# Four loads of v earlier in the batch, z's bounds in one go at the start, and two small first output units in an attention and soft-MoE kernel

## The chip, the cores and the metric

The kernel runs on one core of one Trainium2 chip. The metric is the device time of one execution in microseconds (us), the median of several runs. The core has a matrix engine (TensorE, PE in the profile, its weight loads PEld), a vector engine (VectorE, DVE), a scalar engine (ScalarE, ACT), GpSimd (POOL) and a queue engine (SyncE, SP) that here issues every DMA of the loop. The profile gives for each stretch the clock that was granted to PE, as a share of full speed.

## The reference

```python
B, S, D, DQK = 8, 2496, 256, 64
scores = z @ z.T / S                      # per batch, 2496 x 2496
attn = maximum(scores, 0) ** 2
x = u * (attn @ v)                        # 8 x 2496 x 256, taken as 19968 x 256

logits = x @ phi                          # 19968 x 32: 8 experts with 4 slots each
d = softmax of logits over the tokens     # columns
slot_input = d.T @ x                      # 32 x 256
h = maximum(slot_input[e] @ w1[e], 0)     # per expert, 256 -> 1024
slot_out[e] = h @ w2[e]                   # 1024 -> 256
c = softmax of logits over the slots      # rows
return c @ slot_out                       # 19968 x 256
```

The scores are symmetric, since keys and queries are both z.

## The kernel before

**Steps.** A batch is worked off in 5 chunks of 512 queries (the last has 448), and each chunk in 10 steps of 256 keys. A batch is so 50 steps; the last batch has its chunks in another order and the last chunk in two parts, 60 steps. A step's scores are made two steps ahead by `prepare`: PE multiplies z with z into `sc`, ACT takes the relu and the square (`r`), a copy to 16-bit floats gives the high part `ph` (on ACT or DVE), and DVE's `r` less `ph` gives the low part `pl`. At the step itself PE adds `ph` and `pl` times the high and low part of v into `acc` (`sums_halves`, `sums_whole`).

**Symmetric blocks.** A block of scores that is needed again transposed is transposed by DVE (`y`), stored to DRAM in four DMAs (`turned<-y`, by `store`) and fetched up to seven steps before its use (`r<-turned`, 1 MB, by `fetch`). A block on the diagonal gives half of itself the same way: `lent<-yd` by `lend`, and `rd<-lent` by `borrow`, at most five steps ahead. For such a step ACT copies the fetched half (`ph<-rd`), DVE makes its low part (`pl<-rd,ph`), and DVE then makes both parts of the other half, which is computed.

**The MoE's first half.** The outputs of two chunks (1024 tokens) make a group: its logits `lg`, and moves `xt<-y` in four times four DMAs of 72 KB that bring the group's x into the form in which PE sums it with the exponentials of the logits (`lg<-xt`). The sums of one group are done with the logits of the next one.

**The queue.** Every engine runs its instructions in the order in which the program is written (`InOrder`, so line L74 stands for nearly all of them in the profile; the tiles' names tell them apart). All DMAs of the loop go out on SP in that order, and the n-th waits until the one eight before it has landed. `transfers(h)` writes them down for step h: the load of u, the fetches that come due, loads of the next batch, and the stores that are due.

**Loads of the next batch.** The table `splits` has the steps at which the next batch's z (five tiles `zr`, each 256 KB) and v (ten tiles `vr`, 256 KB each) are loaded. `v_from` holds v's; `v_sq` and `v_at` hold the steps at which ACT takes the squares of a tile and at which ACT and DVE split it in high and low parts. The numbers are compared with h + 2, so a load with the entry 14 goes out in step 12. Twelve buffers (`NRAW`) hold the raw tiles.

**The opening.** Before the loop, batch 0's z is scaled. `measure_z` takes the sums of squares of some tiles of z on DVE (`sq`, into `tops`), `add_bounds` brings them over all partitions with one matmul into the PSUM tile `idle`, and `factors` makes powers of two of them (`norm`, `z_by`). `raise_z` multiplies a tile of z (`cw` in the profile) by its factor. `measure_v` squares tiles of v with a sum along the row (`vq`, into `energy`). `largest` and `scale_v` make v's factors (`v_by`, `few`) of both, with a matmul `idle<-ident,few`. `keep_busy` issues matmuls whose result nobody reads. `prepare_first` is `prepare` in pieces for the first two steps.

**The tail.** After the last batch, the slots' sums are copied into `sT` (a piece of the tile `tiny`), zeroed around them by GpSimd before; the experts' two layers follow (`layer1`, `layer2`), and `tokens(c, u)` makes a unit of the output: 4 groups of 512 tokens (3 in the last) for one half c of the 256 features, on PE into `pf`, copied by ACT and DVE into `ot` and stored with one DMA (`outT`). `UNITS` lists them; the first half of the features goes through them forwards, the second backwards.

Of the kernel before, what the change touches and what calls it, by code (L numbers as in the profile page):

```python
# [18 lines left out]
P = 128  # L19
B, S, D, DQK = 8, 2496, 256, 64  # L20
N = B * S
E_, SE, FF = 8, 4, 1024
NS = E_ * SE
# [3 lines left out]
NQ = 5  # L27
NG = N // 512
NQG = (NG + 1) // 2
UNITS = [(g, min(4, NG - g)) for g in range(0, NG, 4)]  # L30
ROT = S - QC * (NQ - 1)
NP = KT // 4
NBLK = 16
# [44 lines left out]
def attn_soft_moe_kernel(ctx, tc, uT, v, zz, phi, ww, outT):  # L78
    nc = tc.nc

    pe, act, dve, sp = (InOrder(tc, x) for x in (nc.tensor, nc.scalar, nc.vector, nc.sync))
# [14 lines left out]
    raws = moe.enter_context(tc.tile_pool(name="raws", bufs=1))  # L96
# [11 lines left out]
    def pair(name, n):  # L108
        return [cpool.tile([P, n], F32, name=f"{name}{i}") for i in range(2)]

    tops, norm2, z_by, energy, v_by, out_by, few = (
        pair(name, n)
        for name, n in (("tops", NP), ("norm2", NP), ("z_by", NP), ("energy", 2 * NP), ("v_by", 2 * NP), ("out_by", NP), ("few", 4))
    )
# [55 lines left out]
    def load_v(b, i):  # L170
        raw = raws.tile([P, 2, D], F32, tag="raw", name=f"vr_{b}_{i}", bufs=NRAW)
        sp.dma_start(raw, v[b, :, 2 * i : 2 * i + 2, :])
        by = v_by[b % 2][:, i : i + 1]

        def squares():
            sq = raws.tile([P, 512], BF16, tag="vq", name=f"vq_{b}_{i}", bufs=1)
            act.activation(
                sq, raw.rearrange("p t f -> p (t f)"), AF.Square, accum_out=energy[b % 2][:, i : i + 1]
            )

        def high():
            act.activation(vt_[b, i][:, :, 0], raw, AF.Identity, scale=by)

        def low():
            t = vt_[b, i]
            dve.scalar_tensor_tensor(t[:, :, 1], raw, by, t[:, :, 0], op0=ALU.mult, op1=ALU.subtract)

        return squares, high, low
# [36 lines left out]
    z_splits, v_splits, first_z, first_v = {}, [], [], []  # L225
# [15 lines left out]
    one = cpool.tile([1, 1], F32, name="one")  # L241
# [30 lines left out]
    wa = att.enter_context(tc.tile_pool(name="wa", bufs=2, side="right"))  # L272
# [128 lines left out]
    def prepare_first(k):  # L401


        r = wa.tile([P, 2, QC], F32, tag="r", name=f"r_{k}", bufs=4)
        pend[k] = hi, lo = high_low(k)
        ps, _ = scores(k)

        act.activation(r, ps, AF.Relu, scale=2.0**-22)

        def square():  # L410
            if k:
                act.activation(r, r, AF.Square)
            else:
                dve.tensor_mul(r, r, r)

        def high():
            dve.tensor_copy(hi, r)

        def low():
            dve.tensor_sub(lo, r, hi)  # L420

        return square, high, low

    def prepare(k):

# [452 lines left out]
    for b in range(1, B):  # L878
        base, order = (b - 1) * 2 * NP * NQ, BLOCKS[b == B - 1]
        z_at = [28, 29, 30, 31, 39]  # L880
        v_from = [14, 15, 16, 17, 24, 25, 26, 31, 32, 33]
        v_sq = [17, 18, 19, 20, 28, 29, 30, 33, 34, 35]
        v_at = [47, 42, 43, 44, 45, 46, 48, 49, 50, 51]
        for i, (j, at) in enumerate(zip(order, z_at)):
            splits.setdefault(base + 9 + 2 * i, []).append((load_z, b, j, [base + 12 + 2 * i, base + at]))
        for i, (start, sq, at) in enumerate(zip(v_from, v_sq, v_at)):
            splits.setdefault(base + start, []).append(
                (load_v, b, i, [base + sq, base + at, base + at])
            )
# [73 lines left out]
    def measure_v(n):  # L963
        for _ in range(n):
            first_v.pop(0)()

    def measure_z(js):
        for p in range(*js.indices(NP)):
            first_z[p]()
        add_bounds(0, idle, js)  # L970
        factors(0, idle, js)

    measure_z(slice(0, 1))
    raise_z(0)
    keep_busy(1)
    first = prepare_first(0)
    measure_v(2 * NP)
    measure_z(slice(1, 2))
    raise_z(1)
    for f in first:  # L980
        f()
    keep_busy(3)
    measure_z(slice(2, NP))
    keep_busy(3)
    second = prepare_first(1)
    second[0]()
    keep_busy(3)
    largest(0)
    scale_v(0, idle)
    second[1]()  # L990
    split_first_v()
    second[2]()
    split_first_v()
    for p in range(2, NP):
        raise_z(p)
# [44 lines left out]
    x = xg_.pop(q)  # L1040
    mold, sold = runmax[(q + 1) % 2], slot_acc[(q + 1) % 2]

    tiny = wk.tile([P, 2, 1024], F32, tag="xg", name="tiny").rearrange("p a b -> p (a b)")
    sT = tiny[:, 0:512].rearrange("p (c e k) -> p c e k", c=2, k=NS)
    snew = tiny[:, 512 : 512 + D + 1]
    ET = tiny[:, 1024 : 1024 + P]
    fsel = tiny[:, 1280 : 1280 + 2 * NS].rearrange("p (a s) -> p a s", a=2)
# [3 lines left out]
    apart = tiny[:, 1600 : 1600 + P]  # L1051
    E = wk.tile([P, 2 * P], F32, tag="E", name="E_last", bufs=1)[:, 0:P]
    lt = wk.tile([P, 2 * P], F32, tag="L", name="lt_last", bufs=1)[:, 0:P]
    nc.gpsimd.memset(tiny[:, 0:512], 0.0)

    nc.gpsimd.tensor_scalar(
        apart.rearrange("p (t s) -> p t s", s=NS), ssel.unsqueeze(1).to_broadcast([P, 4, NS]),
# [35 lines left out]
    for t, copy, ps in (2, act.copy, xq[:, 0:D]), (3, dve.tensor_copy, xr[:, 0:D]):  # L1093
# [5 lines left out]
        accum_out=mtop,  # L1099
# [18 lines left out]
    sums = [lg[:, 2 * P : 2 * P + NS], pm[:, 2 * P : 2 * P + NS]]  # L1118
# [21 lines left out]
    dve.tensor_sub(l4, l4, spread(0))  # L1140
    slots(snew, 0)
    for c, copy in enumerate((dve.tensor_copy, act.copy)):
        copy(sT[:, c, :, 0:SE], sums[c].rearrange("p (e s) -> p e s", s=SE))
    act.activation(lt, lt, AF.Exp)
    dve.tensor_reduce(rm[:, 1], l4, axis=AX.X, op=ALU.add)
    dve.tensor_scalar_add(rm[:, 1], rm[:, 1], 1e-9)
# [8 lines left out]
    def layer1(i):  # L1155

        ps = sc_ps.tile([P, 512], F32, tag=sc_ps.name, name=f"h_{i}")
        for a in range(2):
            e = 2 * i + a
            for c in range(2):  # L1160
                for g in range(4):
                    pe.matmul(
                        ps[g * NS : (g + 1) * NS, a * D : (a + 1) * D], sT[:, c, e],
                        w_half(2 * e + c, g // 2)[:, g % 2 * D : (g % 2 + 1) * D],
                        start=(c == 0), stop=(c == 1),
                    )
        act.activation(hidden[:, i], ps, AF.Relu)
        return lambda: dve.transpose(hT[i // 2][:, i % 2].rearrange("p a f s -> p (a f s)"), hidden[:, i])
# [39 lines left out]
    second = rest_ps.tile([P, QC], F32, tag="rest_ps", name="po_second")  # L1208
# [3 lines left out]


    op = ctx.enter_context(tc.tile_pool(name="op", bufs=4, reuse_waits="tile"))
    for i in range(3, len(UNITS)):
        split_hi(i)
        split_lo(i)
    soh = op.tile([P, 2, P], F32R, name="soh", bufs=1)
# [24 lines left out]
    def tokens(c, u):  # L1243
        g0, ng = u
        hi, lo = parts[g0 // 4]
        gs = slice(0, ng)
        ot = op.tile([P, 4, 4, P], F32, tag="ot", name=f"ot_{c}_{g0}")
        pf = []
        for i in range(2):
            ps = ring.pop(0)  # L1250
            ring.append(ps)
            pf.append(ps.tile([P, 2, 4, P], F32, tag=ps.name, name=f"pf_{c}_{g0}_{i}"))
        for m, (a, k) in enumerate(((soh, hi), (soh, lo), (sol, hi))):
            for t in range(4):
                rows = slice(t * NS, (t + 1) * NS)
                pe.matmul(
                    pf[t // 2][:, t % 2, :ng], a[rows, c], k[rows, gs],
                    start=(m == 0), stop=(m == 2), tile_position=(t * NS, 0),
                )
        for tp in range(2):  # L1260
            o = ot[:, :ng, 2 * tp : 2 * tp + 2].rearrange("p g t n -> p t g n")
            (dve.tensor_copy if tp else act.copy)(o, pf[tp][:, :, :ng])
        sp.dma_start(
            outT[c * P : (c + 1) * P, g0 * 512 : (g0 + ng) * 512],
            ot[:, :ng].rearrange("p g t n -> p (g t n)"),
        )
# [8 lines left out]
    first = po[0][:, D : D + P]  # L1275
# [3 lines left out]
    parts_out(0, first)  # L1279
    layer2(1, 0, range(2, 3))  # L1280
    left = [(0, f) for f in range(3, 8)] + [(1, f) for f in range(8)]
    units = [(0, u) for u in UNITS] + [(1, u) for u in UNITS[::-1]]
    for i, (c, u) in enumerate(units):
        if i == 7:
            spread_out(1, slots_out(1), po[1][:, D : D + P])
        tokens(c, u)

        for eg, f in [left.pop(0) for _ in range((3, 0, 0, 1, 2, 3, 4)[i] if i < 7 else 0)]:
            layer2(1, eg, [f])
    att.close()  # L1290

# [42 lines left out]
```

## Time and profile before

| what | us |
|---|---|
| three runs | 1298.11, 1301.54, 1307.86 |
| median | 1301.54 |
| the profiled execution, its own time | 1300.08 |
| its span in the trace | 1298.3 |
| mean granted clock of PE | 0.979 |
| the loop's first `acc` starts at | 20.35 |
| the first `outT` DMA is issued at | 1245.45 |

A page of a profile lists the busy time of each engine with its share of the span, then 40 equal slices of the span with the busy share in tenths. In these, the clock and DMA rows of this kernel are:

```profile
PEclk8999999999999999999999999999999999999985
DMA  4868759784888758785787857978487868899869
```

The page further has the chain of work that ended last, followed back from the end, and groups of instructions. A line of a timeline is the start, the duration, the engine, the line, the operation, the tiles written and read, the shape, how many such instructions stand in a row, and in brackets how long the engine had been idle and what it had waited for. A row of the DMA issues gives the number, the size of one and the median time from issue to landing:

```profile
turned<-y SPq DMA_DIRECT2D x320, 256.0 KB, 5.1
r<-turned SPq DMA_DIRECT2D x76, 1024.0 KB, 7.1
xt<-y SPq DMA_DIRECT2D x288, 72.0 KB, 4.1
vr<-in_v SPq DMA_DIRECT2D x80, 256.0 KB, 5.5
```

### The profile page before, as it was taken

The numbers are of one execution on the slowest core, as the hardware profiler recorded it, in microseconds if no ns is written. First come the engines' busy times: TensorE is split into PE (matmuls) and PEld (weight loads), VectorE is DVE, ScalarE is ACT, GpSimd is POOL, SyncE is SP. The second block draws the span as 40 slices with busy tenths as digits, with TensorE's granted clock in tenths as the row PEclk, the third lists the DMA queues.
The fourth block names the chain that finished last, engine by engine and source line by source line (L and its number), as shares of the span: only waits on it lengthen the run. The fifth ranks groups of instructions, "written<-read, shape, count | busy, mean of one in ns | idle before, by whom it ended". The sixth has DMA issues, their size and how long they took to land.

```text
span 1298.3 us, 27660 instructions
## 1 busy us (share of the span) xinstructions
PE 1253.6 (97%) x10965; PEld 607.7 (47%) x10965; DVE 1100.5 (85%) x1588; ACT 934.6 (72%) x1219; POOL 4.2 (0%) x22
## 2 busy tenths in 40 slices
PE   7999999999999999999999999999999999999984
PEld 3444455445544444344544444344554444445752
DVE  6888899789998899689998899788998899886663
ACT  7877797677867798576977678586886778664553
POOL 1000000000000000000000000000000000000000
PEclk8999999999999999999999999999999999999985
DMA  4868759784888758785787857978487868899869
GB/s 139 234 210 245 231 132 278 232 235 145 212 296 240 250 128 233 259 247 169 167 266 231 272 146 193 294 220 260 110 253 248 267 165 218 261 287 295 309 252 381
DMA packets 136402, 298.88 MB, mean 230 GB/s; under 512 B 17872, under 2 KB 38864, under 8 KB 124240
## 3 DMA queue, kind: packets, MB, share of 16 engines
q1 hardware_dynamic: 136272, 297.11, 74.9%
q8 instruction: 86, 1.41, 0.4%
q14 instruction: 44, 0.36, 0.1%
HBM read 162.04 MB, written 113.77 MB: 212 GB/s over the span
## 4 chain that ended last, share of the span: by engine, by line
PE 81%; ACT 5%; DVE 5%; DMA 5%; issue 2%; SPq 1%; DVEq 0%; ACTq 0%; POOLq 0%
PE acc L74 66%; PE sc L74 10%; ACT r L74 3%; PE lg L74 3%; DVE pl L74 2%; PE pf L74 2%; DVE y L74 1%; DMA r<-turned 1%; ACT ot L74 1%; SPq L74 1%; ACT ph L74 1%; DMA xt<-y 1%; ACT v L74 1%; DMA rd<-lent 1%; PE h L74 1%
## 5 line engine op out<-in xcount | busy, mean ns | idle before, releaser
L74 PE MATMUL acc<-ph,v 64*128 64x512 f16 (+5 forms) x5036 | 931.1, 369 | 3.2 <-DVE ph L74 1.2
L74 PEld LDWEIGHTS <-v 64*128 64x128 f16 (+1 forms) x7554 | 469.7, 95 | 527.7 <-issue 39.5
L74 PE MATMUL acc<-pl,v 64*128 64x512 f16 (+5 forms) x2518 | 602.0, 369 | 2.1 <-DVE pl L74 1.8
L74 DVE TENSOR_TENSOR pl<-r,ph 128x1024 f16<-128x1024 f32 (+1 forms) x410 | 467.5, 1146 | 108.5 <-ACT ph L74 81.4
L74 ACT CAST ph<-r 128x1024 f16<-128x1024 f32 (+1 forms) x286 | 289.7, 1018 | 157.1 <-DMA r<-turned 99.4
L74 ACT ACTIVATE r<-sc 128x1024 f32<-128x1024 f32 (+1 forms) x242 | 229.4, 948 | 125.4 <-PE sc L74 122.8
L74 ACT ACTIVATE r<-r 128x1024 f32<-128x1024 f32 (+1 forms) x241 | 237.4, 985 | 6.8
L74 DVE STREAM_TRANSPOSE y<-r 128x1024 f32<-128x1024 f32 x160 | 198.0, 1238 | 0.0
L74 PE MATMUL sc<-z,z 64*128 64x512 f16 x912 | 124.3, 377 | 1.8 <-ACT r L74 1.5
L74 PEld LDWEIGHTS <-z 64*128 64x128 f16 x1380 | 70.2, 94 | 75.9 <-issue 5.8
L74 DVE CAST ph<-r 128x1024 f16<-128x1024 f32 (+1 forms) x124 | 73.9, 596 | 15.5 <-ACT r L74 15.2
L74 DVE SCALAR_TENSOR_TENSOR xg<-acc,out_by,ut 128x1024 f32<-128x1024 f32 (+7 forms) x57 | 51.7, 930 | 11.0 <-PE acc L74 11.0
L74 DVE SCALAR_TENSOR_TENSOR v<-vr,v_by,v 128x512 f16<-128x512 f32 x80 | 58.0, 725 | 0.0
L74 ACT ACTIVATE v<-vr,v_by 128x512 f16<-128x512 f32 x80 | 57.0, 715 | 0.0
L74 PE MATMUL sc<-z 64*128 64x512 f16 (+1 forms) x468 | 50.6, 321 | 0.0
L74 ACT ACTIVATE vq<-vr 128x512 bf16<-128x512 f32 x80 | 49.8, 623 | 0.3
L74 DVE STREAM_TRANSPOSE y<-xg 128x512 f32<-128x512 f32 x72 | 49.4, 687 | 0.0
L74 DVE COPY ot<-pf 128x1024 f32<-128x1024 f32 (+1 forms) x20 | 24.0, 1198 | 20.6 <-PE pf L74 19.8
L74 ACT COPY ot<-pf 128x1024 f32<-128x1024 f32 (+1 forms) x20 | 19.8, 991 | 24.8 <-PE pf L74 20.7
L74 DVE TENSOR_TENSOR pl<-rd,ph 128x512 f16<-128x512 f32 x36 | 24.0, 667 | 10.9 <-ACT ph L74 10.7
L74 ACT CAST ph<-rd 128x512 f16<-128x512 f32 x36 | 21.8, 607 | 13.9 <-DMA rd<-lent 13.7
L74 PE MATMUL lg<-xt 64*32 64x256 f32 x576 | 21.6, 391 | 5.9 <-DMA xt<-y 5.9
(185 smaller groups left out, 536.0 us busy)
## 6 DMA issues: line engine op xcount, KB each, us to landing
turned<-y SPq DMA_DIRECT2D x320, 256.0 KB, 5.1
r<-turned SPq DMA_DIRECT2D x76, 1024.0 KB, 7.1
xt<-y SPq DMA_DIRECT2D x288, 72.0 KB, 4.1
vr<-in_v SPq DMA_DIRECT2D x80, 256.0 KB, 5.5
outT<-ot SPq DMA_DIRECT2D x18, 1024.0 KB, 6.9
ut<-in_uT SPq DMA_DIRECT2D x31, 512.0 KB, 6.2
lent<-yd SPq DMA_DIRECT2D x144, 64.0 KB, 3.0
rd<-lent SPq DMA_DIRECT2D x36, 256.0 KB, 4.8
```

Source lines behind the costliest of these rows:

```text
L74: return lambda *a, **k: self.tc.keep_in_program_order(f(*a, **k))
```

## The change

Three things are changed.

**Loads.** The first four tiles of v of the next batch are loaded at the entries 6 to 9 of the table in place of 14 to 17, so in steps 4 to 7 of the batch before, not in 12 to 15. Their squares and splits stay where they were.

**Opening.** The relu is a piece of `prepare_first` of its own. The scores of step 1 are issued right after the relu of step 0. The squares of z1 to z4 are taken in one go and go through one matmul of four columns, where there were one of one column and one of three. Nine of the ten tiles of v are squared on ACT and the last on DVE. `keep_busy` is called once with 8 instead of three times with 3.

**Tail.** The first output unit of the first feature half is parted in two: 1 group and 3 groups. `tokens` takes its groups from the right place in the parts of the weights. For the second half the unit stays whole. The matmuls of `layer2` that are written between units are handed on by one place. `sT` becomes two tiles, one for each half of the features: one stays in `tiny`, the other is `apart_s`.

```diff
-UNITS = [(g, min(4, NG - g)) for g in range(0, NG, 4)]
+UNITS = [(0, 1), (1, 3)] + [(g, min(4, NG - g)) for g in range(4, NG, 4)]
...
-        def squares():
-            sq = raws.tile([P, 512], BF16, tag="vq", name=f"vq_{b}_{i}", bufs=1)
-            act.activation(
-                sq, raw.rearrange("p t f -> p (t f)"), AF.Square, accum_out=energy[b % 2][:, i : i + 1]
-            )
+        def squares(engine=act):
+            one, to = raw.rearrange("p t f -> p (t f)"), energy[b % 2][:, i : i + 1]
+            if engine is act:
+                sq = raws.tile([P, 512], BF16, tag="vq", name=f"vq_{b}_{i}", bufs=1)
+                act.activation(sq, one, AF.Square, accum_out=to)
+            else:
+                sq = raws.tile([P, 512], BF16, tag="sq", name=f"vq_{b}_{i}", bufs=1)
+                dve.tensor_tensor_reduce(sq, one, one, 1.0, 0.0, op0=ALU.mult, op1=ALU.add, accum_out=to)
...
-        v_from = [14, 15, 16, 17, 24, 25, 26, 31, 32, 33]
+        v_from = [6, 7, 8, 9, 24, 25, 26, 31, 32, 33]
...
     first = prepare_first(0)
-    measure_v(2 * NP)
-    measure_z(slice(1, 2))
+    first[0]()
+    second = prepare_first(1)
+    measure_v(2 * NP - 1)
+    measure_z(slice(1, NP))
+    for f in first[1:]:
+        f()
+    second[0]()
+    second[1]()
     raise_z(1)
-    for f in first:
-        f()
-    keep_busy(3)
-    measure_z(slice(2, NP))
-    keep_busy(3)
-    second = prepare_first(1)
-    second[0]()
-    keep_busy(3)
+    keep_busy(8)
+    first_v.pop()(dve)
     largest(0)
     scale_v(0, idle)
...
+    apart_s = wa.tile([P, 256], F32, tag="yt", name="apart_s", bufs=1)
     tiny = wk.tile([P, 2, 1024], F32, tag="xg", name="tiny").rearrange("p a b -> p (a b)")
-    sT = tiny[:, 0:512].rearrange("p (c e k) -> p c e k", c=2, k=NS)
+    sT = [tiny[:, 0:256].rearrange("p (e k) -> p e k", k=NS), apart_s.rearrange("p (e k) -> p e k", k=NS)]
...
-        gs = slice(0, ng)
+        gs = slice(g0 % 4, g0 % 4 + ng)
...
-    units = [(0, u) for u in UNITS] + [(1, u) for u in UNITS[::-1]]
+    whole = [(0, 4), *UNITS[2:]]
+    units = [(0, u) for u in UNITS] + [(1, u) for u in whole[::-1]]
     for i, (c, u) in enumerate(units):
-        if i == 7:
+        if i == 8:
             spread_out(1, slots_out(1), po[1][:, D : D + P])
         tokens(c, u)
-        for eg, f in [left.pop(0) for _ in range((3, 0, 0, 1, 2, 3, 4)[i] if i < 7 else 0)]:
+        for eg, f in [left.pop(0) for _ in range((0, 3, 0, 0, 1, 2, 3, 4)[i] if i < 8 else 0)]:
             layer2(1, eg, [f])
```

What this moves is shown at three places. The numbers at the end of names count tiles and differ between the two kernels. The first place is SP in batch 3, steps 14 to 21, the stretch that ends with the last moves of `xt`. Before:

```order
L74 DMA r_6673<-turned_0_2_6196 128x2048
L74 DMA zr_3_6675<-in_zz 128x512
L74 DMA vr_1_6677<-in_v 128x512
L74 DMA turned_1_4_6679<-y_6557 32x4x512 x4
L74 DMA vr_2_6721<-in_v 128x512
L74 DMA xt<-y_6275 32x576 x4
L74 DMA r_6770<-turned_1_2_6575 128x2048
L74 DMA zr_4_6772<-in_zz 128x512
L74 DMA vr_3_6774<-in_v 128x512
L74 DMA turned_1_3_6776<-y_6657 32x4x512 x4
L74 DMA xt<-y_6275 32x576 x4
```

After:

```order
L74 DMA r_6673<-turned_0_2_6190 128x2048
L74 DMA zr_3_6675<-in_zz 128x512
L74 DMA turned_1_4_6677<-y_6559 32x4x512 x4
L74 DMA xt<-y_6286 32x576 x4
L74 DMA r_6766<-turned_1_2_6577 128x2048
L74 DMA zr_4_6768<-in_zz 128x512
L74 DMA turned_1_3_6770<-y_6657 32x4x512 x4
L74 DMA xt<-y_6286 32x576 x4
```

Three loads `vr` are gone from among them; the fourth, `vr_0`, stood a few rows earlier. The second place is SP in batch 2, steps 5 to 11, to which loads come. Before:

```order
L74 DMA rd_4263<-lent_0_3987 128x512
L74 DMA xt<-y_3864 32x576 x4
L74 DMA turned_0_3_4310<-y_4201 32x4x512 x4
L74 DMA xt<-y_3864 32x576 x4
L74 DMA zr_0_4416<-in_zz 128x512
L74 DMA turned_0_4_4418<-y_4296 32x4x512 x4
L74 DMA lent_1_4462<-yd_4448 32x4x128 x4
L74 DMA zr_1_4509<-in_zz 128x512
```

After:

```order
L74 DMA rd_4257<-lent_0_3981 128x512
L74 DMA vr_0_4274<-in_v 128x512
L74 DMA xt<-y_3858 32x576 x4
L74 DMA vr_1_4321<-in_v 128x512
L74 DMA turned_0_3_4323<-y_4195 32x4x512 x4
L74 DMA xt<-y_3858 32x576 x4
L74 DMA vr_2_4372<-in_v 128x512
L74 DMA zr_0_4416<-in_zz 128x512
L74 DMA vr_3_4418<-in_v 128x512
L74 DMA turned_0_4_4420<-y_4307 32x4x512 x4
L74 DMA lent_1_4464<-yd_4450 32x4x128 x4
L74 DMA zr_1_4511<-in_zz 128x512
```

The fetch `rd` of `lent_1`, which step 17 uses, follows some rows further down in both, so all four loads are now ahead of it. In batches 3 and 5 no `xt` stands among these rows. The third place is PE in the opening, behind the first scores (`sc_203`); the second scores are `sc_210`:

```order
 L74 MATMUL idle<-const-bfloat16-1.0 128x512
 L74 MATMUL sc_203<-cw 128x512 x2
-L74 MATMUL idle<-tops_80,const-float32-1.0 128x1
+L74 MATMUL sc_210<-cw 128x512 x2
+L74 MATMUL idle<-tops_80,const-float32-1.0 128x4
 L74 LDWEIGHTS const-bfloat16-1.0
```

The second scores stand ahead of the one bounds matmul, where they came after the matmul of three columns and six rounds of `keep_busy`.

More of the change, by code (lines that the diff above doesn't have):

```diff
@@ L406, in prepare_first, with relu @@
         ps, _ = scores(k)
-        act.activation(r, ps, AF.Relu, scale=2.0**-22)
+        def relu():
+            act.activation(r, ps, AF.Relu, scale=2.0**-22)
         def square():
@@ L420, in low @@
             dve.tensor_sub(lo, r, hi)
-        return square, high, low
+        return relu, square, high, low
     def prepare(k):
@@ L976, in attn_soft_moe_kernel @@
     first = prepare_first(0)
-    measure_v(2 * NP)
-    measure_z(slice(1, 2))
-    raise_z(1)
-    for f in first:
-        f()
-    keep_busy(3)
-    measure_z(slice(2, NP))
-    keep_busy(3)
-    second = prepare_first(1)
-    second[0]()
-    keep_busy(3)
+    first[0]()
[6 more added lines that the diff above has]
+    second[1]()
+    raise_z(1)
+    keep_busy(8)
+    first_v.pop()(dve)
     largest(0)
     scale_v(0, idle)
-    second[1]()
+    second[2]()
     split_first_v()
-    second[2]()
+    second[3]()
     split_first_v()
@@ L1053, in attn_soft_moe_kernel @@
     lt = wk.tile([P, 2 * P], F32, tag="L", name="lt_last", bufs=1)[:, 0:P]
-    nc.gpsimd.memset(tiny[:, 0:512], 0.0)
+    nc.gpsimd.memset(tiny[:, 0:256], 0.0)
+    nc.gpsimd.memset(apart_s, 0.0)
     nc.gpsimd.tensor_scalar(
@@ L1142, in attn_soft_moe_kernel @@
     for c, copy in enumerate((dve.tensor_copy, act.copy)):
-        copy(sT[:, c, :, 0:SE], sums[c].rearrange("p (e s) -> p e s", s=SE))
+        copy(sT[c][:, :, 0:SE], sums[c].rearrange("p (e s) -> p e s", s=SE))
     act.activation(lt, lt, AF.Exp)
@@ L1162, in layer1 @@
                     pe.matmul(
-                        ps[g * NS : (g + 1) * NS, a * D : (a + 1) * D], sT[:, c, e],
+                        ps[g * NS : (g + 1) * NS, a * D : (a + 1) * D], sT[c][:, e],
                         w_half(2 * e + c, g // 2)[:, g % 2 * D : (g % 2 + 1) * D],
@@ L1214, in attn_soft_moe_kernel @@
     op = ctx.enter_context(tc.tile_pool(name="op", bufs=4, reuse_waits="tile"))
-    for i in range(3, len(UNITS)):
+    for i in range(3, len(UNITS) - 1):
         split_hi(i)
```

## The prediction

> **What bounds the kernel now.** I read the page's engine shares first, then the chain, then PE's waits, then PE's timeline and windows around the long ones.
>
> ```profile
> span 1298.3 us, 27660 instructions
> ...
> PE 1253.6 (97%) x10965; PEld 607.7 (47%) x10965; DVE 1100.5 (85%) x1588; ACT 934.6 (72%) x1219; POOL 4.2 (0%) x22
> PE 81%; ACT 5%; DVE 5%; DMA 5%; issue 2%; SPq 1%; DVEq 0%; ACTq 0%; POOLq 0%
> PE lg L74 <- DMA xt<-y: 5.9, 2, 3.1
> PE idle L74 <- DVE tops L74: 5.3, 2, 4.6
> ```
>
> PE is the bound: 97% of the span, 81% of the chain. The change adds and removes almost no PE work, so it can win only where PE stands still or runs slowly. Two stalls for `xt` make 5.9 us; the opening's wait for the bounds of z (`tops`) makes another 5.3. What follows the two `xt` stalls is seen in PE's timeline (start, duration, idle time before in brackets) and in windows (busy time of PE, PEld, DVE, ACT, POOL, then granted clock, DMA share, GB/s):
>
> ```profile
> 238.92 0.42 PE L74 MATMUL lg<-xt 64*32 64x256 f32 x8
> 297.83 0.42 PE L74 MATMUL lg<-xt 64*32 64x256 f32 x8
> 538.54 1.50 PE L74 MATMUL lg<-xt 64*32 64x256 f32 x32 [3.08 <-DMA xt<-y]
> 599.38 0.42 PE L74 MATMUL lg<-xt 64*32 64x256 f32 x8
> 839.94 2.52 PE L74 MATMUL lg<-xt 64*32 64x256 f32 x32 [2.83 <-DMA xt<-y]
> ...
> 506.00:526.00 20.00, 20.00 (x142) 9.00 (x137) 18.87 (x27) 15.01 (x20) 0.00 (x0) 1.00 0.99 330
> 536.24:539.65 3.41, 1.11 (x32) 0.74 (x32) 2.52 (x5) 2.37 (x4) 0.00 (x0) 1.00 0.87 247
> 539.65:543.06 3.41, 3.41 (x29) 1.15 (x18) 3.20 (x8) 0.00 (x0) 0.00 (x0) 0.50 0.49 156
> ```
>
> The stalls lie in batches 3 and 5, at the same step. The 20 us before the first are DMA-bound (share 0.99). The window with the stall has PE busy 1.11 of 3.41 us, and the next 3.41 us run at clock 0.50. From the stall's end to the next `lg<-xt` takes 599.38 - 538.54 = 60.84 us; the same work in batch 1, which has no such stall, takes 297.83 - 238.92 = 58.91. So each stall costs its own length plus 1.93 us of slow clock.
>
> **The change part by part. The four loads, batches 3 and 5.**
>
> ```profile
> 480.00:502.00 22.00, 22.00 (x212) 9.98 (x207) 21.58 (x32) 19.18 (x23) 0.00 (x0) 1.00 0.74 181
> 518.00:522.00 4.00, 4.00 (x20) 1.83 (x19) 3.90 (x9) 2.58 (x4) 0.00 (x0) 1.00 1.00 353
> 526.00:528.00 2.00, 2.00 (x11) 0.94 (x10) 1.93 (x5) 0.00 (x0) 0.00 (x0) 1.00 0.22 72
> 516.72 1.24 DVE L74 STREAM_TRANSPOSE y<-r 128x1024 f32<-128x1024 f32 x1
> 528.54 0.43 SPq L74 DMA_DIRECT2D vr<-in_v  x1
> 531.57 5.07 SPq L74 DMA_DIRECT2D xt<-y  x4
> ```
>
> Four loads of 256 KB leave the queue ahead of the last `xt`. At 353 GB/s one is 0.74 us, all four 2.97. They go to 480 to 502, where the DMA engines are busy 0.74 of the time. The last stores before `xt` carry a `y` that was transposed by 516.72 + 1.24, more than 10 us before they go out, so nothing but the queue holds that stretch and it can move up whole. The stalls shrink from 3.08 to 0.11 and from 2.83 to 0, and the slow clock after each goes: (2.97 + 1.93) + (2.83 + 1.93) = 9.7. Ends: nothing more can be had than 9.8; at least 1.5 (2 x 0.74, the load at 528.54 alone), if the hole at 526 to 528 (share 0.22) eats what is saved ahead of it. I take 9.7, since the DMA engines are busy 0.99 of the 20 us up to that hole: bytes set its place, and fewer bytes move it up. [...]
>
> **The same loads, other batches.** There the place they go to is not empty.
>
> ```profile
> 334.00:354.00 20.00, 20.00 (x192) 10.60 (x190) 19.00 (x26) 17.83 (x20) 0.00 (x0) 1.00 0.86 214
> 368.20 0.60 ACT L74 CAST ph<-rd 128x512 f16<-128x512 f32 x1
> 371.55 0.65 DVE L74 TENSOR_TENSOR pl<-rd,ph 128x512 f16<-128x512 f32 x1
> 372.57 0.69 DVE L74 TENSOR_TENSOR pl<-r,ph 128x512 f16<-128x512 f32 x1
> 373.82 0.38 PE L74 MATMUL acc<-pl,v 128*128 128x512 f16 x1
> 220.51 0.62 ACT L74 CAST ph<-rd 128x512 f16<-128x512 f32 x1 [1.40 <-DMA rd<-lent]
> 221.55 0.65 DVE L74 TENSOR_TENSOR pl<-rd,ph 128x512 f16<-128x512 f32 x1
> 224.67 0.38 PE L74 MATMUL acc<-pl,v 128*128 128x512 f16 x1
> ```
>
> Behind the new loads on SP stand moves of `xt`, stores `turned`, and the fetch `rd` of a diagonal piece; its readers are ACT `ph<-rd`, DVE `pl<-rd`, DVE's other half and at last PE. The shift of `rd` lies between 0 (a fifth of 20 us is free by the 0.86: 2.8 us) and 2.97 plus four issues of 0.43 = 4.7. I take 2.7, near the loads' own time, because SP takes the next DMA only as earlier ones land. Cover in batch 2: DVE comes 371.55 - 368.80 = 2.75 after ACT is done, and PE takes the second half 373.82 - 373.26 = 0.56 after DVE: 3.31 in all. So no stall there, nor in 4 and 6. Batch 1 has 221.55 - 221.13 = 0.42, and with DVE's other half ending 1.71 after 221.55, as in batch 2, 224.67 - 223.26 = 1.41: 1.83 in all. It loses 2.7 - 1.83 = 0.9 (0 to 2.9). In batch 0 the loads go out ahead of its first fetches too; PE's waits name no DMA there, so I count nothing, on that cover alone. The squares and splits of v stay at their steps, so the earlier arrival itself gains nothing.
>
> **The opening.**
>
> ```profile
> 6.92 1.02 ACT L74 ACTIVATE r<-sc 128x1024 f32<-128x1024 f32 x1 [4.69 <-PE sc L74]
> 7.79 0.49 DVE L74 TENSOR_SCALAR cw<-cw,z_by 128x512 f32<-128x512 f32 x1
> 8.19 1.22 DVE L74 TENSOR_TENSOR r<-r 128x1024 f32<-128x1024 f32 x1
> 10.17 1.23 DVE L74 TENSOR_TENSOR pl<-r,ph 128x1024 f16<-128x1024 f32 x1
> 12.77 0.69 DVE L74 CUSTOM_DVE_ANT_0 sq<-cw 128x512 bf16<-128x512 f32 x1
> 13.52 0.59 PE L74 MATMUL idle<-tops,const-float32-1.0 128*128 128x3 f32 x2 [4.63 <-DVE tops L74]
> 15.49 0.17 DVE L74 TENSOR_SCALAR v_by<-energy 128x10 int32<-128x10 int32 x1 [0.77 <-ACT vq L74]
> 15.60 1.94 PE L74 MATMUL sc<-cw 64*128 64x512 f32 x4
> 18.39 0.29 DVE L74 TENSOR_REDUCE few<-idle 128x2 f32<-128x128 f32 x1 [2.33 <-PE idle L74]
> 20.35 0.39 PE L74 MATMUL acc<-ph,v 64*128 64x512 f16 x2 [0.57 <-ACT v L74]
> ```
>
> Before, `few` has its input late because PE runs the second scores (15.60 to 17.54) ahead of it. Now those follow the first relu: 7.94 + 1.94 = 9.9; the one bounds matmul 0.59 more, 10.5; three small DVE operations, 0.17 each as `v_by` (15.49) and their wait, 0.6, 11.1; square, `ph`, `pl` of half 0 take 11.40 - 8.19 = 3.2, 14.3; raising z1 0.49, 14.8; the last v's square, now DVE's, 0.69 as `sq` and a read of its sum, 15.6. DVE now waits there for the last v's landing, with `v_by` and `few` behind it; ACT had squared that v before 15.49, so it is there by 14.8. So `v_by` starts as at 15.49, but PE is free: three DVE operations (0.5), the matmul and its wait (0.5), and `few` is reduced at 16.7, not 18.39. That is 1.7 off, the first `acc` at 18.65. The keep-busy matmuls (8 rounds in one go for 9 in three) follow the bounds matmul at 10.5 and are done by about 14 (8 pairs of 0.39, as the pair at 20.35), so PE idles some 2 of the next 3.4 us, and a window like that was followed by half clock above. The loop's first us would then lose about 1.1; at even odds I deduct 0.5. Net 1.2 gained (0.3 lost clock wholly and a late v, to 2.4 with the second scores at full clock).
>
> **The tail.**
>
> ```profile
> 1244.17 1.23 DVE L74 COPY ot<-pf 128x1024 f32<-128x1024 f32 x1 [0.78 <-PE pf L74]
> 1245.45 25.18 SPq L74 DMA_DIRECT2D outT<-ot  x12
> 1250.00:1294.00 44.00, 27.87 (x278) 15.43 (x276) 20.59 (x18) 17.15 (x19) 0.00 (x0) 0.62 1.01 418
> ```
>
> The output stream is DMA-bound to the end (1.01 at 418 GB/s), so only its start counts. A 256 KB first unit could go out at most 1.28 earlier (1245.45 - 1244.17), and holds 0.63 us of stream; the next unit, 768 KB, can't be ready before the old first one was, and a further pair of copies stands ahead of it. I take half of 0.63, 0.3 gained (-0.4 to 1.3); the parting of `sT` into two tiles is in it, hidden behind copies of 0.2.
>
> Sum: 9.7 - 0.9 + 1.2 + 0.3 = 10.3 less, from the profiled execution's 1300.08 (its span of 1298.3 and 1.8 around it): 1289.8. That execution lies 1.46 under the median 1301.54; against the median it is 0.9% less.
>
> **The rivals.**
> - The loads cost more where they now stand (slower). If each takes its 256 KB at that stretch's own 214 GB/s, 1.22 us, `rd` comes 4.9 later. Batches 2, 4, 6 stall 4.9 - 3.31 = 1.6 and, if the clock falls behind it, lose 1.93 more; batch 1 loses 3.1 + 1.93. That is 3 x 3.5 + 5.0 = 15.6 against the 0.9 counted: 1304.5. It decides from a shift of 3.8, provided the clock falls each time. Against it: the share there is 0.86, so bytes are not yet the limit.
> - The same without the clock, at a shift of 4.0: 3 x 0.7 + 2.2 = 4.3 against 0.9, 1293.2.
> - The loads are not what holds `xt`: the hole at 526 to 528 stays where it is, only 0.74 comes back per stall, and the clock still falls: 1289.8 + 9.7 - 1.5 = 1298.0. For it: a share of 0.22 in the midst of a full queue. Against it: `xt` is behind all four in one queue.
> - The slow stretches stay without the stalls (or a third reason sets the clock): 3.9 less gained, 1293.7. [...]
>
> **How the numbers follow.** Chances: forecast 0.63; loads not the cause 0.14; shift without clock 0.12; clock unmoved 0.05; slower 0.06. The forecast's own range is 1286.5 to 1291.5 (opening and tail at their good ends; batch 1 at its bad one). To 1298.5 the cases at 1293 and 1298 are in; what is left out is the slower rival and tails. About 1% (1288.5 or 1314.6) is what a measurement of this kernel can tell from no change. The forecast lies 1.3 short of the lower bound; four tenths of its chance fall beyond it, 0.25, and with the noise of three runs I say 0.3 for faster by more than 1%. Slower by more than 1% needs the first rival at its worst: 0.04.
>
> **What would show it.** Right: no wait of `lg` for `xt` over 0.5 us in batches 3 and 5, and granted clock 1.00 through 530 to 545; `ph<-rd` later by 2 to 3 us in even batches with PE not waiting for `pl`; a wait for `pl` under 1 us in batch 1 near 224; the first `acc` near 18.6; the first `outT` about 1 us earlier against the copies' start, its end moved by less than 0.5. Wrong: PE waits for `pl` or `ph` at step 17 of batches 2, 4, 6; a wait for `xt` above 2 us left; half clock in the loop at another place.

## The result, and the profile after

| | before | changed |
|---|---|---|
| median of 20 runs, us | 1301.7 | 1295.66 |
| lowest to highest | 1298.11 to 1308.36 | 1293.92 to 1299.94 |
| ratio | | 0.9944, 95% interval 0.9934 to 0.9954 |
| the profiled execution | 1300.08 | 1299.94 |

The change takes 6.0 us off the median; 11.7 were forecast against the first median, 10.3 against the profiled execution. The profiled execution of the changed kernel was the longest of its 20, so the two profiles hardly differ in span, and what the change does must be read stretch by stretch. The page and PE's waits after:

```profile
span 1298.2 us, 27694 instructions
PE 1260.7 (97%) x10973; PEld 611.3 (47%) x10973; DVE 1100.8 (85%) x1588; ACT 932.1 (72%) x1218; POOL 4.2 (0%) x23
...
PE sc L74 <- ACT r L74: 4.8, 12, 1.1
PE idle L74 <- DVE few L74: 2.0, 1, 2.0
...
PE lg L74 <- DMA xt<-y: 0.9, 1, 0.9
...
PE idle L74 <- DVE tops L74: 0.9, 1, 0.9
```

The wait for `xt` fell from 5.9 us to 0.9, the one for `tops` from 5.3 to 0.9. New are 2.0 for `few`, and the waits for ACT's relu ahead of scores are 4.8 (1.8 before). PE is busy 7.1 us longer with nearly the same work: the two stretches at half clock behind the stalls are gone, but others have come, in the opening and in the tail (below). In PE's timeline (start, duration, ...) and the windows (PE, PEld, DVE, ACT, POOL, granted clock, DMA share, GB/s) the two old stalls now read:

```profile
539.57 0.77 PE L74 MATMUL lg<-xt 64*32 64x256 f32 x9 [0.94 <-DMA xt<-y]
838.89 1.69 PE L74 MATMUL lg<-xt 64*32 64x256 f32 x32
...
526.00:528.00 2.00, 2.00 (x11) 0.88 (x9) 2.00 (x4) 2.00 (x5) 0.00 (x0) 1.00 0.68 221
528.00:530.00 2.00, 2.00 (x12) 0.88 (x9) 1.90 (x6) 0.34 (x2) 0.00 (x0) 1.00 0.34 74
530.00:532.00 2.00, 2.00 (x11) 0.94 (x10) 2.00 (x5) 0.00 (x0) 0.00 (x0) 1.00 0.70 174
537.28:540.70 3.42, 2.48 (x68) 1.22 (x64) 2.37 (x4) 3.39 (x5) 0.00 (x0) 1.00 0.82 216
```

One wait is down to 0.94. The other is no longer listed, though its two steps still take 0.92 too long (the table below). No half clock follows either. Counted from its batch's first `acc`, the first of them starts at 539.57 - 469.15 = 70.42 against 538.54 - 465.97 = 72.57 before: 2.15 earlier, not 2.97. The hole in the DMA engines' work ahead of it is still there and wider (0.68, 0.34 and 0.70 in six microseconds, where it was 0.22 in two, with 0.93 and 0.85 on its sides).

The opening after, in timeline and windows:

```profile
6.11 2.08 PE L74 MATMUL sc<-cw 64*128 64x512 f32 x4 [0.29 <-DVE cw L74]
8.23 1.02 ACT L74 ACTIVATE r<-sc 128x1024 f32<-128x1024 f32 x1 [6.00 <-PE sc L74]
9.31 2.08 PE L74 MATMUL sc<-cw 64*128 64x512 f32 x4 [1.12 <-ACT r L74]
11.31 0.59 PE L74 MATMUL idle<-tops,const-float32-1.0 128*128 128x4 f32 x2
15.94 0.68 DVE L74 CUSTOM_DVE_ANT_0 vq<-vr 128x512 bf16<-128x512 f32 x1
16.74 0.17 DVE L74 TENSOR_SCALAR v_by<-energy 128x10 int32<-128x10 int32 x1
17.46 0.44 PE L74 MATMUL idle<-ident,few 64*128 64x64 f32 x4 [1.97 <-DVE few L74]
17.93 0.29 DVE L74 TENSOR_REDUCE few<-idle 128x2 f32<-128x128 f32 x1 [0.62 <-PE idle L74]
19.68 0.61 PE L74 MATMUL acc<-ph,v 64*128 64x512 f16 x2 [0.70 <-ACT v L74]
...
15.09:18.51 3.42, 1.45 (x12) 0.55 (x8) 2.56 (x10) 2.74 (x5) 0.00 (x0) 1.00 0.02 6
18.51:21.92 3.41, 2.53 (x12) 0.70 (x12) 3.32 (x7) 2.98 (x4) 0.00 (x0) 0.50 0.00 0
21.92:25.33 3.41, 3.30 (x18) 0.91 (x14) 3.41 (x7) 2.60 (x4) 0.00 (x0) 0.50 0.02 5
```

The chain runs as forecast, but the first scores take 2.08 here, and the relu ends at 9.25 instead of 7.94; everything behind is later by about as much (`v_by` 16.74 for 15.6, `few` 17.93 for 16.7, `acc` 19.68 for 18.65). Then PE is idle for 1.97 of a window of 3.41 us, and two windows at half clock follow: the first step takes 5.71, where it took 3.46.

In the other batches and the tail:

```profile
224.37 0.62 ACT L74 CAST ph<-rd 128x512 f16<-128x512 f32 x1 [3.68 <-DMA rd<-lent]
372.44 0.62 ACT L74 CAST ph<-rd 128x512 f16<-128x512 f32 x1 [2.00 <-DMA rd<-lent]
...
437.36 0.82 PE L74 MATMUL sc<-z 64*128 64x512 f16 x6 [0.40 <-ACT r L74]
730.26 0.82 PE L74 MATMUL sc<-z,z 64*128 64x512 f16 x6 [0.76 <-ACT r L74]
...
426.23 1.04 ACT L74 CAST ph<-r 128x1024 f16<-128x1024 f32 x1 [2.25 <-DMA r<-turned]
...
1241.13 49.86 SPq L74 DMA_DIRECT2D outT<-ot  x21
...
1240.00:1244.00 4.00, 3.77 (x52) 2.46 (x52) 1.56 (x3) 1.17 (x2) 0.00 (x0) 0.56 0.19 70
1244.00:1248.00 4.00, 3.32 (x26) 1.86 (x26) 1.23 (x1) 1.13 (x2) 0.00 (x0) 0.50 0.56 229
```

Against the batch's first `acc`, `ph<-rd` comes 51.15 - 48.86 = 2.3 later in batch 1 (batch starts 173.22 and 171.65) and 51.47 - 49.39 = 2.1 later in batch 2 (320.97 and 318.81); batch 1 pays 0.6 and batch 2 nothing at that place. But batches 2 and 4 lose 1.0 and 2.05 at steps 35 to 37, a place that the prediction did not speak of: ACT has waited for a turned block there (2.25 at 426.23), and PE then waits for ACT's relu. In the tail the first `outT` goes out early, and then the DMA engines wait for units that PE makes at half clock.

### The profile page after: what moved, and what is told of

The parts are those of the page before. It is cut to its first block, busy times and chain, and to the rows that moved or that the text cites. A ratio compares the mean times of both kernels' runs of the same rounds, so it can differ in the third digit from the quotient of the medians.

```text
span 1298.2 us, 27694 instructions
## 1 busy us (share of the span) xinstructions
PE 1260.7 (97%) x10973; PEld 611.3 (47%) x10973; DVE 1100.8 (85%) x1588; ACT 932.1 (72%) x1218; POOL 4.2 (0%) x23
## 4 chain that ended last, share of the span: by engine, by line
PE 74%; ACT 8%; DMA 7%; DVE 6%; issue 2%; SPq 2%; ACTq 0%; DVEq 0%; POOLq 0%
PE acc L74 59%; PE sc L74 9%; ACT r L74 4%; PE lg L74 2%; SPq L74 2%; PE pf L74 2%; DMA r<-turned 2%; DVE y L74 2%; DMA turned<-y 2%; DVE pl L74 2%; ACT ph L74 2%; DMA rd<-lent 1%; ACT ot L74 1%; ACT v L74 1%; DMA vr<-in_v 1%
## 5 line engine op out<-in xcount | busy, mean ns | idle before, releaser
L74 DVE COPY ot<-pf 128x1024 f32<-128x1024 f32 (+2 forms) x21 | 24.1, 1149 | 24.8 <-PE pf L74 24.8
L74 ACT COPY ot<-pf 128x1024 f32<-128x1024 f32 (+2 forms) x21 | 20.0, 951 | 28.7 <-PE pf L74 28.7
L74 DVE SCALAR_TENSOR_TENSOR z<-zr,z_by,z 128x512 f16<-128x512 f32 x35 | 25.8, 738 | 0.0
```

The lines of the kernel that those rows point to most:

```text
L74: return lambda *a, **k: self.tc.keep_in_program_order(f(*a, **k))
```

## The experiments

Each kernel was timed in five rounds against the kernel before on the same chip (which took 1301.08 to 1302.25 in these rounds; the 1301.7 belongs to the second row), and profiled once, so the columns behind the median show single executions. This table has the ratios and what the profiled executions show, all in us: the start of the first `acc`; the duration of the first step; what batch 1 and batches 2 and 4 together take above 147.16 each; what steps 21 and 22 of batches 3 and 5 take above the 8.48 of batch 1; and the time from the experts' first layer (`h`) to the last landing of `outT`. Nearly all of what batches 2 and 4 lose lies at steps 35 to 37; only in the run of the loads alone 0.73 of it lies at steps 16 and 17 of batch 4. The loads column says in which batches the four loads go out early.

| kernel | ratio (95%) | median | loads | first acc | step 0 | b 1 | b 2+4 | steps 21, 22 of b 3, b 5 | h to end |
|---|---|---|---|---|---|---|---|---|---|
| before | | 1301.7 | none | 20.35 | 3.46 | 0.0 | 0.0 | 5.23, 4.99 | 67.96 |
| changed | 0.9944 (0.9934 to 0.9954) | 1295.66 | all | 19.68 | 5.71 | 0.59 | 3.07 | 1.50, 0.92 | 71.10 |
| changed, again | 0.9951 (0.9931 to 0.9971) | 1295.37 | all | 19.66 | 5.75 | 1.16 | 4.44 | 1.09, 0.65 | 68.12 |
| loads only | 0.9939 (0.9916 to 0.9962) | 1294.5 | all | 21.72 | 3.46 | 1.46 | 2.89 | 0.74, 1.69 | 68.02 |
| opening only | 1.0002 (0.9987 to 1.0018) | 1301.2 | none | 19.77 | 4.84 | 0.0 | 1.84 | 6.56, 3.54 | 67.94 |
| tail only | 1.0018 (1.0001 to 1.0035) | 1304.38 | none | 21.92 | 3.46 | 0.0 | 0.0 | 3.66, 3.00 | 68.22 |
| loads, all but 3 and 5 | 1.0010 (0.9994 to 1.0026) | 1302.92 | not 3, 5 | 22.39 | 3.46 | 1.23 | 1.04 | 3.36, 1.95 | 67.97 |
| loads, 3 and 5 | 0.9941 (0.9924 to 0.9958) | 1293.04 | 3, 5 | 21.83 | 3.46 | 0.0 | 0.0 | 0.86, 0.30 | 68.00 |
| the same with z | 0.9948 (0.9928 to 0.9969) | 1293.96 | 3, 5 | 20.36 | 3.46 | 0.0 | 1.08 | 0.16, 0.19 | 67.94 |
| opening, 12 rounds | 0.9984 (0.9971 to 0.9996) | 1298.92 | none | 19.63 | 3.46 | 0.0 | 0.0 | 4.90, 4.33 | 68.03 |
| units only | 1.0000 (0.9986 to 1.0014) | 1302.19 | none | 21.74 | 3.46 | 0.0 | 0.0 | 5.43, 6.58 | 68.15 |
| sT only | 1.0001 (0.9985 to 1.0016) | 1302.38 | none | 21.98 | 3.46 | 0.0 | 2.21 | 5.33, 5.60 | 67.99 |
| loads and opening, 12 rounds | 0.9930 (0.9912 to 0.9948) | 1293.08 | all | 19.88 | 3.46 | 1.69 | 0.25 | 0.12, 1.07 | 68.03 |
| loads and z in 3 and 5, opening, 12 rounds | 0.9915 (0.9897 to 0.9932) | 1291.3 | 3, 5 | 19.80 | 3.46 | 0.0 | 0.1 | 0.22, 0.11 | 67.95 |

**The changed kernel again**, with no edit.

> The changed kernel once more. Its profiled execution took 1299.94 us, the longest of its 20 runs (median 1295.66), so another execution is wanted. If what the profile showed at steps 35 to 37 of batches 2 and 4 (1.0 and 2.0 us) belongs to the change, it shows again and the span stays near 1298; if it belongs to that execution, batches 2 and 4 come back to 147.2 each. The ratio to the kernel before should be 0.994 to 0.996 in any case.

The losses in batches 2 and 4 were there again (4.4), and the first step took 5.75; the tail was back at 68.12. So the half clock in the opening and the losses were no chance of one execution. The 3.1 of the tail did not come again.

**Each part alone.** Loads:

```diff
-        v_from = [14, 15, 16, 17, 24, 25, 26, 31, 32, 33]
+        v_from = [6, 7, 8, 9, 24, 25, 26, 31, 32, 33]
```

> Only the four loads moved. My theory: they carry the gain, 7 to 9 us (ratio 0.993 to 0.9945), with the waits for xt in batches 3 and 5 below 1 us and no half clock behind them, and 0.6 lost at step 16 of batch 1. Rival, that the even batches pay for it: waits at steps 35 to 37 of batches 2 and 4, ratio 0.996 or more.

The loads carry the gain: 0.9939, some 7.9 us of 1301. Both waits for `xt` are short (1.10 the longer), no half clock follows, and batch 1 pays 1.46. The losses at steps 35 to 37 that the rival named are there too, 1.11 in batch 2 and 1.05 in batch 4, without the ratio that it gave. Batch 4 loses another 0.73 at steps 16 and 17: there `ph<-rd` comes 3.7 later against the batch's first `acc` than in the kernel before, past the cover of 3.31 that the prediction worked out, and PE waits.

The opening, the diff being the two pieces of the change on `prepare_first` with its calls and on `squares`:

```diff
     first = prepare_first(0)
-    measure_v(2 * NP)
-    measure_z(slice(1, 2))
+    first[0]()
+    second = prepare_first(1)
+    measure_v(2 * NP - 1)
+    measure_z(slice(1, NP))
...
+    keep_busy(8)
+    first_v.pop()(dve)
```

> Only the opening changed. My theory: the first acc comes 0.7 to 1.7 earlier, but PE idles before the loop, the first step runs at half clock and takes some 5.7 us for 3.5, so that nothing is gained or up to 1.5 us lost (ratio 1.000 to 1.0015). Rival, that the half clock was chance of one execution: the first acc 0.7 to 1.7 earlier and the first step 3.5, ratio 0.9985 to 0.9995.

Nothing gained: the first `acc` is early, the first step takes 4.84. The slow first step came another way here than in the two profiles of the changed kernel. In those the clock rose at 15.09 and 15.79 and fell again one window later, with PE idle for 1.97 and 2.06 us of that window. Here it had not risen at all: the second `sc<-cw` of the chain still takes 2.08 at 9.14 and the next 2.06 at 17.74, and the clock is first full at 23.66. This run also had 1.84 in batches 2 and 4, with no load moved.

The tail, with the pieces of the change on `UNITS`, `tokens` and `sT`:

```diff
+UNITS = [(0, 1), (1, 3)] + [(g, min(4, NG - g)) for g in range(4, NG, 4)]
...
+    sT = [tiny[:, 0:256].rearrange("p (e k) -> p e k", k=NS), apart_s.rearrange("p (e k) -> p e k", k=NS)]
```

> Only the first output unit in two and sT in two tiles. My theory: the stream of outT starts 1 us earlier but has a hole behind the small units, and ends where it ended: ratio 0.9995 to 1.0005. Rival, that the earlier start is kept: 0.9990. Rival, that the units bring half clock earlier in the tail: 1.001 to 1.002.

The ratio is above 1, 1.0018; from `h` to the end it is 68.22 against 67.96.

**Where the loads gain and where they cost.** The loads moved in all batches but 3 and 5, then in 3 and 5 alone (the table serves the batch after, so 4 and 6):

```diff
-        v_from = [14, 15, 16, 17, 24, 25, 26, 31, 32, 33]
+        v_from = [*([14, 15, 16, 17] if b in (4, 6) else [6, 7, 8, 9]), 24, 25, 26, 31, 32, 33]
```

> Loads moved in batches 0, 1, 2, 4 and 6, not in 3 and 5. My theory: what these batches lose comes from the moved loads, through fetches that land later: 1.5 at steps 16 and 17 of batch 1, 1.0 to 2.5 at steps 35 to 37 of batch 2, 1.5 to 2.0 in batch 4, and the two stalls for xt stay: ratio 1.002 to 1.004. Rival: the losses at steps 35 to 37 came by chance of the execution (the run with the opening alone had them too): batch 1 loses its 0.6 to 1.5, batches 2 and 4 nothing, ratio 1.000 to 1.001.

```diff
-        v_from = [14, 15, 16, 17, 24, 25, 26, 31, 32, 33]
+        v_from = [*([6, 7, 8, 9] if b in (4, 6) else [14, 15, 16, 17]), 24, 25, 26, 31, 32, 33]
```

> Loads moved in batches 3 and 5 alone. My theory: the gain of the loads without the losses of the other batches: the waits for xt at 0.7 to 1.7 us, no half clock behind them, batches 1, 2 and 4 at 147.2 each, ratio 0.990 to 0.992, better than the 0.9939 of all loads moved. Rival (losses by chance): as with all loads, 0.993 to 0.995.

Batch 1 pays where its loads are moved (0.59 to 1.69 in five profiles) and never else (0.0 in nine): settled. With the loads moved everywhere but in 3 and 5 the gain is gone: 1.0010, the rival's ratio. With those of 3 and 5 alone it stays: 0.9941, again the rival's ratio and not the 0.990 to 0.992 of the theory. Against the 0.9939 of all loads no difference can be told, though 3 us would have been at the edge of what the intervals tell. In the profiles neither theory stands alone: batches 2 and 4 lost 0.25 to 4.4, 2.3 on the mean, in the five that move their loads, and 0 to 2.2, 0.6 on the mean, in the nine that don't (and batch 6 lost 1.6 in one). Moving the loads seems to bring such losses oftener; five executions don't settle it.

**Is it bytes that set the last `xt`?** The loads of z moved too, in batches 3 and 5:

```diff
+        z_from = [8, 9, 10, 10, 11] if b in (4, 6) else [9, 11, 13, 15, 17]
         for i, (j, at) in enumerate(zip(order, z_at)):
-            splits.setdefault(base + 9 + 2 * i, []).append((load_z, b, j, [base + 12 + 2 * i, base + at]))
+            splits.setdefault(base + z_from[i], []).append((load_z, b, j, [base + 12 + 2 * i, base + at]))
```

> As before, and in batches 3 and 5 the five loads of z also go out in steps 6 to 9. If bytes set the place of the last xt, the two or three z loads gone from the stretch ahead of it (0.74 each) take away the 0.7 to 1.7 left: no wait of lg for xt over 0.3, ratio 0.001 below that of the loads in batches 3 and 5 alone. If the time in which the DMA engines idle behind the xt moves sets it, the wait stays at 0.5 or more and the ratio the same.

PE's waits name no `xt` any more, and steps 21 and 22 are within 0.2 of batch 1's, as the first theory said. But the size does not fit it. Counted from the batch's first `acc`, the last `xt` lands at 69.35 and 69.49, against 69.97 and 69.51 with the loads of v alone: 0.6 and 0.0 earlier, where two or three loads of 0.74 would make 1.5 to 2.2. And steps 21 and 22 come to 0.12 and 0.30 with v's loads alone too (batch 3 of all loads with 12 rounds, batch 5 of the loads in 3 and 5). So it is not shown that bytes alone set the place of the last `xt`. The ratio, 0.9948, can't tell a difference of 0.4 a batch.

**The half clock in the opening:**

```diff
-    keep_busy(8)
+    keep_busy(12)
```

> The changed opening alone, with 12 rounds of keep_busy in place of 8. If PE's 1.7 to 2.0 us of idle time ahead of the second factors' matmul is what brings half clock to the first step, filling it with four more rounds (0.43 each) takes most of that idle time away, the first step returns to 3.5 from 4.8 to 5.75 us and the ratio is 0.9985 to 0.9995. If the half clock is set elsewhere, the first step stays above 4.8 and the ratio at 1.000.

PE's wait for `few` falls from 1.70 (1.97 in the changed kernel) to 0.38. The clock rises at 16.51; the window that begins there has PE idle for 1.25, where it was 1.97 in the changed kernel's first full window, and the clock stays:

```profile
16.51:19.92 3.41, 2.16 (x16) 0.65 (x10) 2.45 (x12) 2.38 (x4) 0.00 (x0) 1.00 0.00 0
19.92:23.34 3.42, 2.91 (x28) 1.13 (x28) 3.42 (x7) 3.36 (x5) 0.00 (x0) 1.00 0.00 0
```

The first step is back at 3.46, here and in the two other profiles with 12 rounds (below), where it was 4.84 to 5.75 in three with 8. The ratio is 0.9984, that is 2.1 us, against 1.0002 with 8 rounds; the two intervals still overlap.

**The two halves of the tail:**

```diff
+UNITS = [(0, 1), (1, 3)] + [(g, min(4, NG - g)) for g in range(4, NG, 4)]
```

> Only the first output unit in two. My theory: from the start of the experts' first layer the first outT goes out 1.1 earlier, the second unit does not land earlier than the old first one did by more than a few tenths, and the end comes 0 to 0.3 later: ratio 0.9995 to 1.0005 by that, and up to 1.002 if half clock sets in earlier in the tail, as in the profiled execution of the changed kernel. Rival: all of the tail's 1.0018 comes from sT, then 1.000 here.

```diff
+    sT = [tiny[:, 0:256].rearrange("p (e k) -> p e k", k=NS), apart_s.rearrange("p (e k) -> p e k", k=NS)]
```

> Only sT in two tiles. My theory: nothing, 0.9995 to 1.0005, since the two copies are 0.2 each and the wait of the first layer for the second stays at 0.4. Rival: the wait for the zeroing or for the second tile grows, 1.001 or more and a longer wait of h.

1.0000 and 1.0001: neither does anything that can be measured, and the 1.0018 of both together is not explained by them. From `h` to the end the parted unit takes 68.12 to 68.22 in three profiles, 0.15 to 0.25 more than the whole one on the mean (67.94 to 68.03 in ten). In the fourth, the first of the changed kernel, it takes 71.10, with half clock from 14.4 us after `h`; in no other profile does half clock come there before 20. Whether the parted unit brings that now and then, one in four can't tell.

**Put together**, first with all loads, then with those of batches 3 and 5 alone (and z's there too), both without the tail. Against the changed kernel, with `sT` and `tokens` as before too:

```diff
-    keep_busy(8)
+    keep_busy(12)
...
-UNITS = [(0, 1), (1, 3)] + [(g, min(4, NG - g)) for g in range(4, NG, 4)]
+UNITS = [(g, min(4, NG - g)) for g in range(0, NG, 4)]
```

> All loads moved, the changed opening with 12 rounds of keep_busy, the tail as before. If the parts add up, 0.9939 x 0.9984: 0.992 to 0.993, against 0.9944 and 0.9951 for the changed kernel as it is.

> Loads of v and z moved in batches 3 and 5 alone, the opening with 12 rounds, the tail as before. If what the moved loads cost in batches 1, 2 and 4 (1.1 + 1.1 + 1.7 by the profiles, less the 0.8 that such stalls take without them) is real, this is 2 to 4 us below the kernel with all loads moved: 0.990 to 0.992. If those losses are chance, the two are alike.

0.9930, near the product of the parts (0.9923), and 0.9915 (1291.3 us, 11 below the kernel before): the best of all that ran. Its five runs (1290.41 to 1291.53) all lie below the six of the other (1292.4 to 1293.83), which speaks for a cost of the loads in batches 1, 2 and 4, though the two intervals overlap and the kernels also differ in z's loads. Those may have a price as well: batches 3 and 5 lose 1.0 and 0.45 at steps 16 and 17 here, and at most 0.1 in the other run with z moved. PE is busy 7.9 us less than in the changed kernel's first profile, and 0.8 less than in the kernel before:

```profile
span 1289.7 us, 27659 instructions
PE 1252.8 (97%) x10969; PEld 607.0 (47%) x10969; DVE 1100.3 (85%) x1587; ACT 933.7 (72%) x1217; POOL 4.2 (0%) x22
```

## Why the prediction was right and where it was off

The direction, the cause and the main mechanism were right, and 1295.66 lies in the range; the size was not: 6.0 gained on the medians (7.3 by the ratio) of 10.3 forecast. Of the signs that the prediction gave, four missed in the profile: a wait for `xt` of 0.94 was left where 0.5 was the most, half clock came in the loop at another place, its first step, the first `acc` is at 19.68 for 18.6, and the end of `outT` moved by 3.1 (by 0.2 in the other three with the parted unit).

**Loads, batches 3 and 5: right, mis-sized.** The term was 9.7. Over the executions, steps 21 and 22 took 4.6 too long on the mean (14 stalls with the loads in their old place, 1.95 to 6.58) and 0.9 with the loads moved (10, 0.12 to 1.69): 3.7 a batch, 7.4 together. Two things in it were off. The whole stretch does not move up by the bytes taken away: the last `xt` came 2.15 earlier, not 2.97, while the DMA engines' hole widened. Over all profiles it lands 72.5 us after its batch's first `acc` with the loads in their old place and 70.1 with them moved, 2.4 earlier. The bound from below, the load behind the hole alone, was too low, and the value taken too high. And the slow clock was counted behind every stall, on two of two in one profile. Of the 14 it followed 9: that both of the first profile had it was chance. The run of the tail alone has a stall of 3.09, as long as the others, and no half clock; the run of sT alone has one:

```profile
534.88:538.29 3.41, 2.12 (x44) 0.78 (x38) 2.09 (x2) 3.41 (x7) 0.00 (x0) 1.00 1.03 388
538.29:541.71 3.42, 1.62 (x36) 0.87 (x38) 2.53 (x5) 1.69 (x2) 0.00 (x0) 1.00 0.77 204
541.71:545.12 3.41, 3.41 (x34) 1.52 (x32) 2.51 (x8) 1.48 (x2) 0.00 (x0) 1.00 0.51 154
...
538.43:541.84 3.41, 0.45 (x10) 0.36 (x18) 2.53 (x4) 2.65 (x5) 0.00 (x0) 1.00 0.80 222
541.84:545.25 3.41, 3.41 (x41) 1.37 (x27) 3.17 (x7) 0.00 (x0) 0.00 (x0) 0.50 0.68 234
```

In the first, the stall falls on two windows, with PE idle 1.29 and 1.80 in them; in the second nearly all of it (2.96) falls in one.

**Loads, batch 1: right.** 0.9 forecast, 1.2 on the mean of five; `rd` came 2.3 later for 2.7 forecast in the first profile, and 2.6 later on the mean of five against nine. **Even batches at step 17: right but for one.** `rd` came 1.7 to 2.1 later on the means, with 3.3 of cover, and the cover held in 14 of 15 batches; in batch 4 of the loads alone it came 3.7 later and cost 0.73. **Not foreseen:** steps 35 to 37 of batches 2 and 4, part of which comes without the loads too. I had looked for the loads' cost in the stretch to which they go and in the next fetch, not twenty steps on. What links the two was not found: the queue's order there is the same before and after.

**The opening: the chain right, the deduction too small.** The first `acc` is at 19.7 on the mean of six kernels with the new opening and 21.5 of eight with the old one (20.35 to 22.39): 1.8 gained, 1.7 forecast. The old profile had a lucky start, 20.35, so the 18.65 worked out from it was a microsecond early. The half clock behind it was put at about 1.1 with even odds, 0.5; the slow first step came in each of the three executions with 8 rounds and cost 1.4 to 2.3. Net nothing, where 1.2 were forecast.

**The tail: wrong.** 0.3 forecast, 0.15 to 0.25 lost, and 3.1 in one execution. The first `outT` goes out 1.1 earlier after `h`, but the statement that only the start of the stream counts fell: behind the first small unit the DMA engines run out of work. Even without the early half clock their share is 0.56 to 0.58 from 16 to 17 us after `h` and 0.28 to 0.33 from 17 to 18, where the whole unit, which goes out later, has 1.08 to 1.15 from 17 to 18.

**The sum.** The parts as the profiles have them (7.4 less 1.2, less 2.3 - 0.6 in batches 2 and 4, nothing in the opening, 0.2 lost in the tail) make 4.3 gained; the runs say 6.0 to 7.3. For the loads of batches 3 and 5 alone the two agree, 7.4 and 7.7. The rest is not assigned: single profiled executions scatter by more than that, between 4.5 us below and 4.3 above their kernel's median.

Of the rivals, the one that the loads are not what holds `xt` fell with the two kernels that move them alone; the one that the slow stretches stay fell with the stalls' end, as half clock follows in none of the ten places with moved loads, though its 1293.7 is the nearest of all to 1295.66. The slower one fell: the fetch was 1.7 to 2.6 late on the means, not 3.8, and came near that once. The one of a shift without the clock gave 1293.2; what the even batches lost, they lost at another place than it named.

## What to carry to other kernels

Where a transfer ends a wait, count what stands ahead of it in its queue, and move that to a stretch with room; but take the gain of a queue's bytes with a discount where its engines show a hole (here the last `xt` came 2.15 earlier for 2.97 of bytes, with shares of 0.68, 0.34 and 0.70 ahead of it). A clock penalty seen behind two stalls in one profile is a chance, not a price (over the profiles here it followed 9 of 14): look at several executions before it goes into a sum. When engines are given more to do side by side at the start, look whether PE's own waiting then costs the clock (the three profiles with 8 rounds had a first step of 4.84 to 5.75 for 3.46); a few idle matmuls were worth some 2 us here, and without them the reordering itself was worth nothing.

## What was not expected of the hardware

- In the first profiles of both kernels the granted clock changed only at moments a whole number of 3.413 us apart. The stretches between two changes last 3.413, 10.240, 522.239, 3.413, 296.960, 3.413, 406.186, 6.827 and 10.240 us in the profile before, and 3.413, 6.827, 1215.145, 17.067 and 6.827 in that of the changed kernel. The first change came at 3.75 in the one and at 15.09 in the other, which is 3.32 such windows apart, so their place differed between the two executions.
- Half clock did not follow each long wait of PE. In the 14 profiles, between 100 us and the tail, twelve windows at full clock were followed by half clock, with PE idle for 1.80 to 2.97 us of their 3.41: among them 2.30 at 536.24 and 2.83 at 836.61 in the kernel before, 2.96 at 538.43 in the run of sT alone, 1.80 at 1125.39 in the run of the tail alone. Every window with 1.88 or more was followed by it; of the five with 1.75 to 1.82 one was (1.80 at 538.29 in the run of the tail alone, 1.81 at 839.44 in that of the opening alone and 1.77 at 1120.50 in that of the loads and the opening were not), and none with less. The stall of 3.09 that fell on two windows, with 1.29 and 1.80 in them, cost no clock. The openings do not sort themselves by this idle time: 1.22 at 3.75 in the kernel before was followed by half clock, 1.25 at 16.51 in the run with 12 rounds was not. What decides it was not shown.
- The time from start to the first `acc` of the same opening differs by 2.0 us between executions (20.35 to 22.39). In the two earliest (the kernel before, 20.35, and the loads of 3 and 5 with z, 20.36), the clock was full from 3.8 to 7.2 us, while the first scores ran.
- In eight of the profiles batch 2, 4 or 6 loses 0.44 to 0.46 and 0.59 at steps 36 and 37, nearly the same figures each time, in 7 of 15 batches with moved loads and 5 of 27 without; what decides in which execution and batch is open.
